# Seven products in the second layer of the fourth and fifth 512-row block of four more rounds, with the sums kept in quarters of the hidden tile

## The chip, the cores and the metric

The kernel runs on one core of a Trainium2 chip. The metric is the device time in microseconds (us) of one execution; the median of several is compared. Within the core, PE is TensorE (matrix products), DVE is VectorE, ACT is ScalarE, POOL is GpSimd and SP is SyncE, which here only issues transfers.

## What is computed

The input x has 8 batches of 2496 rows of 256 numbers. Each batch goes through a two-dimensional Fourier transform of which the real part is kept; then each of the 19968 rows is given to one of eight experts, and passes through that expert's two layers:

```python
X = np.fft.fft(x, axis=1)
X = np.fft.fft(X, axis=2)
x = X.real.reshape(B * S, D)
logits = x @ w_gate
expert_idx = np.argmax(logits, axis=1)
...
h = np.maximum(x_sorted[lo:hi] @ w1[e], 0.0)
y_sorted[lo:hi] = h @ w2[e]
...
return gate_w[:, None] * y
```

D is 256, there are 8 experts, and the hidden width F is 1024. All of it is in fp32. gate_w is the softmax probability of the chosen expert.

## The kernel before

**Stages.** Per batch, `first` folds and transforms along the sequence, `regroup` and `second` finish the transform, `route` picks the expert of each row and its place, and `send` scatters rows (with GpSimd's indirect transfers) into a buffer in HBM, `Xs`, sorted by expert. The experts work on blocks of rows of one expert. The blocks come in rounds (`rounds`, L132): round 0 has two of 256 and four of 128 rows, round 1 four of 256, round 2 three of 512, rounds 3 to 6 five of 512 each, round 7 five of 512, then seven of 256 and twenty-one of 128. While round b works, the transform of batch b+1 is woven in.

**The order of the work.** All engines run in the order in which the program issues. The main loop (L954 to 982) takes one step of `experts` at a time; each step reports a share of work, and per share some steps of the transform (`side`) and some scatters are issued. From round 3 on, transform steps are dealt only in the second layer of a block (the first reports `full`), and so fast that they are used up about three fifths through the round; the fourth and fifth block have PE to themselves. Scatters of `send` are still issued in the fourth block. A block counts 15 units, 7 in the first and 8 in the second layer, whichever way the second is done.

**Seven products.** From round 3 on, `seven` (L610) makes the first layer of a 512-row block, and of the 256-row blocks of round 7, by seven products of quarters in place of eight (Strassen's scheme in Winograd's form). The weights' side needs four differences (`Left`, L555), the rows' side four (`right`, L571, called from `turn`, L580). Per half of the hidden quarters (g is 0 or 1; one pass for 256 rows) the products go to five banks of PSUM, a to e, in the order 0, 5, 6, 4, 1, 3, 2. ACT copies bank a into p1, DVE adds: u2 = p1 + b, u3 = u2 + d, h22 = u3 + c, h21 = u3 + e, h12 = u2 + c; h11 is bank a after product 1. ACT takes the maximum with zero of each. The hidden tile hT has one buffer. Between the evictions, `step` takes one piece of pending DVE work: first the block's `chores`, then the next block's `Left`.

**The second layer.** Plain blocks (L840 to 851) take each 128 rows in turn: eight products of 128x128 by 128x256 into bank b or d, then ACT scales by the gate (L849) and POOL scatters the rows to the output. In round 7 the 512- and 256-row blocks take `lower` (L657): again seven products, now with the hidden quarters on the left and quarters of the second weights on the right. What it needs of the hidden side (s1, s2, s4 and the difference of h22 and h21) are four `chores` per half, made after the maximum, in tiles that share buffers with the input's (tag "xq"). The differences of the second weights are made by `below` (L605) in the block before, by POOL for a 512-row block and by DVE for a 256-row one. Sums p1, u2, u3 and the output y have tiles of their own. Which blocks take it, `quartered` (L197) says: all `halved` blocks of round 7.

The expert's weights (1 MB a layer) are loaded per block by SP, up to three blocks ahead; rows are fetched for the next two. The first layer's input of the next block is turned (DVE transposes, ACT negates, DVE makes the four differences) during the second layer of the block before.

## Time and profile before

| | |
|---|---|
| median of 3 runs | 1286.0 us (1285.17 to 1287.41) |
| the profiled execution: its time | 1297.33 us |
| its span, first to last instruction | 1295.5 us |
| granted TensorE clock, mean | 0.971 |
| output tiles scaled in plain blocks (L849) | 129, 473 ns each |
| scatters to the output / into Xs | 163 / 160, about 1.0 us each on POOL |
| HBM traffic over the span | 193 GB/s |

The profile is of one execution. Its busy times say how long each engine had an instruction in work; a group of instructions is named by its line, engine and tiles, with count and mean. A matrix product appears as two records. L222 is the helper through which nearly all products are issued, so these groups are told apart by the tiles' names: a to e are the banks of the seven products, ph and py those of plain first and second layers. "The chain" is the work followed back from the last instruction, at each step to what released it. Lines quoted with a start, a length and a name are from the chain or from the instructions in order of time.

### The profile page before, as it was taken

To read this page: it belongs to the slowest core of one execution; us is meant where nothing else is said; L and a number is where in the kernel's file an instruction comes from. 1 tells how busy PE (TensorE), PEld (TensorE's weight loads), DVE (VectorE), ACT (ScalarE), POOL (GpSimd) and SP (SyncE) were. 2 spreads that over 40 slices of the span, in tenths; PEclk is the share of its full clock that TensorE was granted. 3 is DMA by queue.
4 is the path that set the end of the run, shared out by engine and by line. 5 is a ranking of instruction groups with operands and counts; after the bars stand their busy time and mean duration, and the time that the engine had idled before them with its cause. 6 is when DMAs were issued, how large, how long until landed. Compare 5 with 4: busy or idle time off the path is not lost.

```text
span 1295.5 us, 20735 instructions
## 1 busy us (share of the span) xinstructions
PE 1237.7 (96%) x7003; PEld 1090.5 (84%) x7003; DVE 700.5 (54%) x1772; ACT 423.4 (33%) x1059; POOL 360.6 (28%) x355
## 2 busy tenths in 40 slices
PE   6769899899999999999999999999999999999997
PEld 4658788687688888888888888888889999999996
DVE  4554145244256655566356655467488774444662
ACT  1423133132244333443234333343333332222222
POOL 0244304314411531135111531145364221111112
PEclk6869999999999999999999999999999999999998
DMA  8877857726636853456433744344355237777776
GB/s 240 275 237 270 310 205 254 276 84 201 201 114 176 277 152 110 141 150 242 120 102 127 241 128 149 98 135 146 107 151 164 90 113 288 276 265 273 290 294 241
DMA packets 134023, 249.75 MB, mean 193 GB/s; under 512 B 85065, under 2 KB 99891, under 8 KB 114332
## 3 DMA queue, kind: packets, MB, share of 16 engines
q1 hardware_dynamic: 117143, 203.33, 48.3%
q0 software_dynamic: 15888, 42.14, 9.0%
q10 hardware_dynamic: 885, 2.94, 0.7%
q8 instruction: 57, 0.93, 0.3%
q14 instruction: 50, 0.41, 0.1%
HBM read 194.97 MB, written 54.83 MB: 193 GB/s over the span
## 4 chain that ended last, share of the span: by engine, by line
PE 70%; issue 18%; DMA 4%; POOL 3%; DVE 2%; another core or an unknown queue 2%; ACT 1%; SPq 0%; POOLq 0%; ACTq 0%; DVEq 0%
PE py L222 28%; PE a L222 7%; PE c L222 7%; PE ph L222 6%; PE p L222 5%; PE d L222 4%; PE b L222 4%; PE s L222 3%; PE e L222 3%; POOL out_dram L237 3%; DMA xq<-in_x_dram 2%; PE pt L595 1%; DMA Xs<-rows,pi 1%; DMA xb<-Xs 0%
## 5 line engine op out<-in xcount | busy, mean ns | idle before, releaser
L222 PE MATMUL py<-w_sb,hT 128*128 128x256 f32 x2016 | 455.9, 381 | 6.5 <-DVE hT L808 3.9
L222 PEld LDWEIGHTS py<-w_sb,hT 128*128 128x128 f32 x2016 | 379.5, 191 | 57.2 <-DVE hT L808 4.3
L237 POOL DMA_INDIRECT out_dram<-y,ro x163 | 160.8, 986 | 729.2 <-ACT y L849 497.9
L237 POOL DMA_INDIRECT Xs<-rows,pi x160 | 163.3, 1020 | 198.3 <-ACT pi L469 103.6
L222 PE MATMUL ph<-xT,w_sb 128*128 128x128 f32 (+2 forms) x992 | 172.4, 329 | 8.5 <-DVE hT L808 6.7
L222 PEld LDWEIGHTS ph<-xT,w_sb 128*128 128x128 f32 x992 | 136.1, 193 | 34.1 <-issue 17.2
L849 ACT ACTIVATE y<-py,xb 128x256 f32<-128x256 f32 x129 | 61.0, 473 | 313.5 <-PE py L222 271.6
L222 PE MATMUL a<-xT,w_sb 128*128 128x256 f32 (+1 forms) x512 | 117.5, 356 | 0.0
L808 DVE TENSOR_SCALAR hT<-ph 128x512 f32<-128x512 f32 x43 | 29.7, 691 | 161.9 <-issue 79.7
L633 DVE TENSOR_TENSOR u<-p,b 128x512 f32<-128x512 f32 x57 | 39.2, 687 | 132.9 <-PE b L222 96.7
L222 PEld LDWEIGHTS a<-xT,w_sb 128*128 128x128 f32 x512 | 89.2, 190 | 10.3 <-issue 0.2
L643 ACT ACTIVATE hT<-a 128x512 f32<-128x512 f32 x57 | 34.0, 597 | 151.2 <-PE a L222 133.6
L410 DVE COPY lg<-p 128x16 f32<-128x16 f32 x80 | 13.9, 174 | 121.0 <-ACT zs L407 117.5
L222 PE MATMUL s<-xq,w 104*112 104x256 f32 (+2 forms) x208 | 62.9, 427 | 11.1 <-DVE xq L299 10.9
L810 ACT ACTIVATE hT<-ph 128x512 f32<-128x512 f32 x55 | 32.8, 597 | 98.2 <-PE ph L222 71.0
L222 PEld LDWEIGHTS p<-table,t 120*128 120x128 f32 x352 | 54.3, 204 | 12.3 <-issue 6.6
L222 PE MATMUL p<-table,t 120*128 120x120 f32 (+1 forms) x352 | 58.2, 290 | 3.8 <-issue 2.7
L222 PE MATMUL c<-xT,ws 128*128 128x256 f32 (+1 forms) x256 | 59.1, 358 | 2.3 <-issue 1.7
L222 PE MATMUL p<-table,zz 128*128 128x145 f32 (+1 forms) x320 | 56.8, 302 | 3.8 <-issue 2.0
L222 PE MATMUL d<-xT,w_sb 128*128 128x256 f32 (+1 forms) x256 | 58.8, 357 | 0.0
L222 PE MATMUL e<-xs,w_sb 128*128 128x256 f32 (+1 forms) x256 | 58.7, 356 | 0.0
L222 PE MATMUL b<-xs,ws 128*128 128x256 f32 (+1 forms) x256 | 58.7, 356 | 0.0
(148 smaller groups left out, 1739.1 us busy)
## 6 DMA issues: line engine op xcount, KB each, us to landing
w_sb<-in_moe_w_dram SPq DMA_DIRECT2D x132, 1024.0 KB
xq<-in_x_dram SPq DMA_DIRECT2D x24, 896.0 KB
xb<-Xs SPq DMA_DIRECT2D x100, 128.0 KB
Td<-t SPq DMA_DIRECT2D x18, 448.0 KB
t<-Td SPq DMA_DIRECT2D x8, 768.0 KB
t<-Td SPq DMA_DIRECT2D x8, 640.0 KB
xb<-Xs SPq DMA_DIRECT2D x25, 129.0 KB
Td<-t ACTq DMA_DIRECT2D x6, 448.0 KB
```

Source lines behind the costliest of these rows:

```text
L222: nc.tensor.matmul(o, lhsT=lhsT, rhs=rhs, start=start, stop=stop, **kw)
L237: return unordered(pool.indirect_dma_start(out=dst, out_offset=bass.IndirectOffsetOnAxis(ap=idx, axis=0), in_=rows, in_offset=None, bounds ...
L410: vec.tensor_copy(lg[:, k:k + 2], p3[:, NY:NY + 2 * E].rearrange("p (m e) -> p m e", m=2))
L595: nc.tensor.transpose(pt[:, c, t], xb[:, 2 * h + t, c:D:2], ident[:])
L633: vec.tensor_tensor(u2[:], p1[:], b[:], op=add)
L643: act.activation(h11, a[:], ACTF.Relu)
L808: vec.tensor_scalar(o, ph[:], 0.0, None, op0=ALU.max)
L810: act.activation(o, ph[:], ACTF.Relu)
L849: act.activation(y[:], py[:], ACTF.Copy, scale=meta[:, i, 1:2])
```

## The change

- `quartered` now also takes the position of a block in its round: the fourth and fifth 512-row block of rounds 3 to 6 make the second layer by seven products as well. That is eight blocks more than the twelve of round 7.
- In `seven`, for every block that uses it, p1, u2 and u3 have no tiles any more: they are put where h11, h12 and h21 come to lie later. In a quartered block h21 isn't passed through ACT's maximum; DVE takes it in a fused operation that makes s1 and the difference of h21 and h22 (whose sign is turned; the weights' difference with it). s2 is then written over h22 once product 0 of the second layer has read it, and s4 over h12 once product 1 has.
- `below` becomes the class `Below`. Its four differences are made in the block itself, one after each of the first four products of its first layer, by POOL for 512 rows and DVE for 256.
- In `lower` the sums p1, u2, u3 live in the halves of the output tiles. The next block's input is turned after s4, u2 and u3 instead of at three fixed steps, and bank b is added after product 4 instead of after product 6. A last bare yield is added.
- Output tiles y are three pairs of 128 rows in place of six single ones, for all blocks. The planner's tiles have one buffer in place of two, but for `gone`.

```diff
-def quartered(b, size):
-    return halved(b, size) and b == B - 1
+def quartered(b, size, at):
+    return halved(b, size) and (b == B - 1 or at >= 3)
...
-            return cp.tile([1, *dims], dt, tag="p_" + name, name="p_" + name, bufs=2)
+            return cp.tile([1, *dims], dt, tag="p_" + name, name="p_" + name, bufs=2 if name == "gone" else 1)
...
-    def below(w, eng):
-        ws2 = sp.tile([128, 3, FC // 2, H], F32, tag="t4", name="ws2")
-        return right(ws2, *(w[:, 4 * f:4 * f + 4, k * H:(k + 1) * H] for f in (1, 0) for k in range(2)), eng=eng)
-    def seven(size, l, r, hT, step, after):
+    class Below:
+        def __init__(self, w, eng):
+            ws2 = bp.tile([128, 3, FC // 2, H], F32, tag="ws2", name="ws2", bufs=1)
+            o = [ws2[:, k] for k in range(3)]
+            b11, b12, b21, b22 = (w[:, 4 * f:4 * f + 4, k * H:(k + 1) * H] for f in (1, 0) for k in range(2))
+            self.eng, self.all = eng, (b11, b21, b22, o[2], o[0], o[1], b12)
+            self.due = deque([(o[0], b12, b11), (o[1], b22, o[0]), (o[2], b21, o[1]), (b12, b12, b22)])
+        def step(self):
+            if self.due:
+                o, p, q = self.due.popleft()
+                self.eng.tensor_tensor(o, p, q, op=sub)
+    def quarters(hT, size):
+        th, half = size // 2, FC // 2
+        return [hT[:, k * half:(k + 1) * half, t * th:(t + 1) * th] for k in range(2) for t in range(2)]
+    def seven(size, l, r, hT, both, step, ends):
...
         for g in range(half // fp):
             a, b, c, d, e = (pse.tile([128, fp, th], F32, tag=k, name=k) for k in "abcde")
-            p1, u2, u3 = (bp.tile([128, fp, th], F32, tag=n, name=n, bufs=1) for n in ("p1", "u2", "u3"))
-            h11, h12, h21, h22 = (hT[:, k * half + g * fp:k * half + (g + 1) * fp, t * th:(t + 1) * th]
-                                  for k in range(2) for t in range(2))
+            h11, h12, h21, h22 = (q[:, g * fp:(g + 1) * fp] for q in quarters(hT, size))
             product(g, 0, a)
-            act.copy(p1[:], a[:])
+            act.copy(h11, a[:])
             yield
             product(g, 5, b)
-            vec.tensor_tensor(u2[:], p1[:], b[:], op=add)
+            vec.tensor_tensor(h12, h11, b[:], op=add)
             yield
             product(g, 6, d)
-            vec.tensor_tensor(u3[:], u2[:], d[:], op=add)
+            vec.tensor_tensor(h21, h12, d[:], op=add)
             yield
             product(g, 4, c)
-            vec.tensor_tensor(h22, u3[:], c[:], op=add)
+            vec.tensor_tensor(h22, h21, c[:], op=add)
             step()
             yield
             product(g, 1, a, False)
@@ -644,17 +657,20 @@
             act.activation(h22, h22, ACTF.Relu)
             yield
             product(g, 3, e)
-            vec.tensor_tensor(h21, u3[:], e[:], op=add)
-            act.activation(h21, h21, ACTF.Relu)
+            vec.tensor_tensor(h21, h21, e[:], op=add)
+            if not both:
+                act.activation(h21, h21, ACTF.Relu)
             yield
             product(g, 2, c, False)
-            vec.tensor_tensor(h12, u2[:], c[:], op=add)
+            vec.tensor_tensor(h12, h12, c[:], op=add)
             act.activation(h12, h12, ACTF.Relu)
-            after(h11, h12, h21, h22, slice(g * fp, (g + 1) * fp))
+            ends(g)
             step()
             yield
...
-        p1, u2, u3 = (bp.tile([128, nt, H], F32, tag=n, name=n, bufs=1) for n in ("p1", "u2", "u3"))
+            for i in range(nt):
+                act.activation(y[k][:, i, lo:hi], y[k][:, i, lo:hi] if src is None else src[:, i], ACTF.Copy,
+                               scale=gate[:, k * nt + i])
+
+        def plus(o, p):
+            vec.tensor_tensor(o, o, p[:], op=add)
         a, b, c, d = (bank(k) for k in "abcd")
-        one, two = y[:, nt:2 * nt], y[:, 0:nt]
+        p1, u2, u3, high = (y[k][:, 0:nt, h * H:(h + 1) * H] for k, h in ((1, 0), (1, 1), (0, 0), (0, 1)))
         product(0, a)
-        act.copy(p1[:], a[:])
+        act.copy(p1, a[:])
+        s2()
+        if nt == 1:
+            turn_some()
         yield
         product(3, b)
         yield
         product(1, a, False)
+        s4()
+        step()
+        turn_some()
+        yield
+        product(5, c)
+        vec.tensor_tensor(u2, p1, c[:], op=add)
         scaled(1, 0, H, a)
+        if nt == 2:
+            turn_some()
+        yield
+        product(6, d)
+        vec.tensor_tensor(u3, u2, d[:], op=add)
         step()
-        yield
-        product(5, c)
-        vec.tensor_tensor(u2[:], p1[:], c[:], op=add)
-        yield
-        product(6, d)
-        vec.tensor_tensor(u3[:], u2[:], d[:], op=add)
-        vec.tensor_tensor(two[:, :, 0:H], u3[:], b[:], op=add)
-        step()
+        turn_some()
         yield
         c = bank("c")
         product(4, c)
-        vec.tensor_tensor(two[:, :, H:], u3[:], c[:], op=add)
-        vec.tensor_tensor(u2[:], u2[:], c[:], op=add)
+        vec.tensor_tensor(high, u3, c[:], op=add)
+        plus(u3, b)
+        plus(u2, c)
         scaled(0, 0, D)
-        send_rows(0, nt)
+        send_rows(0)
         step()
         yield
         d = bank("d")
         product(2, d)
-        vec.tensor_tensor(one[:, :, H:], u2[:], d[:], op=add)
+        plus(u2, d)
         scaled(1, H, D)
-        send_rows(nt, 2 * nt)
+        send_rows(1)
         step()
         yield
+        yield
...
-            both = quartered(b, size)
+            both = quartered(b, size, at)
+            below = None
             if both:
-                th, r2 = size // 2, rest
-                s12 = xp.tile([128, 2, FC // 2, th], F32, tag="xq", name="s12", bufs=3)
-                s4 = xp.tile([128, FC // 2, th], F32, tag="xq", name="s4", bufs=3)
-                l2 = [hT[:, 4 * f:4 * f + 4, t * th:(t + 1) * th] for t, f in ((1, 1), (1, 0))]
-                l2 += [s4, hT[:, 0:4, 0:th], s12[:, 0], s12[:, 1], hT[:, 4:8, 0:th]]
-
-            def after(h11, h12, h21, h22, at):
+                s1 = bp.tile([128, FC // 2, size // 2], F32, tag="s1", name="s1", bufs=1)
+                h11, h12, h21, h22 = quarters(hT, size)
+                below = Below(w2_sb, pool if size == BIG else vec)
+                fp = 1024 // size
+                parts = [slice(lo, lo + fp) for lo in range(0, FC // 2, fp)]
+
+            def ends(g):
                 if both:
-                    for o, p, q, op in ((s12[:, 0, at], h21, h11, add), (s12[:, 1, at], s12[:, 0, at], h22, sub),
-                                        (h21, h22, h21, sub), (s4[:, at], h12, s12[:, 1, at], sub)):
-                        chores.append(lambda o=o, p=p, q=q, op=op: vec.tensor_tensor(o, p, q, op=op))
+                    part = parts[g]
+                    for o, q, op in ((s1, h11, add), (h21, h22, sub)):
+                        chores.append(lambda o=o[:, part], p=h21[:, part], q=q[:, part], op=op:
+                                      vec.scalar_tensor_tensor(o, p, 0.0, q, op0=ALU.max, op1=op))
 
             if halved(b, size):
-                for _ in seven(size, left.all, xT, hT, step, after):
+                for _ in seven(size, left.all, xT, hT, both, step, ends):
+                    if both:
+                        below.step()
                     yield 0.5, True
                 while chores:
...
-                if follow[1] == BIG and quartered(*follow[:2]):
-                    rest = below(got[0][1], pool)
             if both:
-                y = xp.tile([128, BIG // 128, D], F32, tag="t1", name="y4")
-
-                def send_rows(lo, hi):
-                    for i in range(lo, hi):
-                        put_row(out, ro[:, i:i + 1], y[:, i], NT - 1, "out")
-
-                for i, _ in enumerate(lower(size, l2, r2, y, meta[:, :, 1:2], send_rows,
-                                            left.step if follow and halved(*follow[:2]) else lambda: None)):
-                    if i in (0, 2, 4):
-                        xT = next(turned, xT)
+                y = [bp.tile([128, 2, D], F32, tag="y", name="y", bufs=3) for _ in range(2)]
+
+                def send_rows(k):
+                    for i in range(n // 2):
+                        row = k * n // 2 + i
+                        put_row(out, ro[:, row:row + 1], y[k][:, i], NT - 1, "out")
+
+                def turn_some():
+                    nonlocal xT
+                    xT = next(turned, xT)
+
+                def s2():
+                    for part in parts:
+                        vec.tensor_tensor(h22[:, part], s1[:, part], h22[:, part], op=sub)
+
+                def s4():
+                    for part in parts:
+                        vec.tensor_tensor(h12[:, part], h12[:, part], h22[:, part], op=sub)
+
+                for _ in lower(size, (h22, h12, h12, h11, s1, h22, h21), below.all, y, meta[:, :, 1:2], send_rows,
+                               turn_some, s2, s4, left.step if follow and halved(*follow[:2]) else lambda: None):
                     yield 1, False
-                n = 0
-            for i in range(n):
+            for i in range(0 if both else n):
                 xT = next(turned, xT)
                 py = pse.tile([128, D], F32, tag="bd"[i % 2], name="py")
...
-                y = bp.tile([128, D], F32, tag="y", name="y", bufs=6)
-                act.activation(y[:], py[:], ACTF.Copy, scale=meta[:, i, 1:2])
-                put_row(out, ro[:, i:i + 1], y[:], NT - 1, "out")
+                if i % 2 == 0:
+                    y = bp.tile([128, 2, D], F32, tag="y", name="y", bufs=3)
+                act.activation(y[:, i % 2], py[:], ACTF.Copy, scale=meta[:, i, 1:2])
+                put_row(out, ro[:, i:i + 1], y[:, i % 2], NT - 1, "out")
...
-            if follow and follow[1] == BLK and quartered(*follow[:2]):
-                rest = below(got[0][1], vec)
```

More of the change, by code (lines that the diff above doesn't have):

```diff
@@ L646, in seven, with lower @@
             product(g, 3, e)
-            vec.tensor_tensor(h21, u3[:], e[:], op=add)
-            act.activation(h21, h21, ACTF.Relu)
+            vec.tensor_tensor(h21, h21, e[:], op=add)
+            if not both:
+                act.activation(h21, h21, ACTF.Relu)
             yield
             product(g, 2, c, False)
-            vec.tensor_tensor(h12, u2[:], c[:], op=add)
+            vec.tensor_tensor(h12, h12, c[:], op=add)
             act.activation(h12, h12, ACTF.Relu)
-            after(h11, h12, h21, h22, slice(g * fp, (g + 1) * fp))
+            ends(g)
             step()
             yield
-    def lower(size, l, r, y, gate, send_rows, step):
+    def lower(size, l, r, y, gate, send_rows, turn_some, s2, s4, step):
         nt = size // 256
@@ L672, in scaled @@
         def scaled(k, lo, hi, src=None):
-            for i in range(k * nt, (k + 1) * nt):
-                act.activation(y[:, i, lo:hi], y[:, i, lo:hi] if src is None else src[:, i - k * nt], ACTF.Copy,
-                               scale=gate[:, i])
-        p1, u2, u3 = (bp.tile([128, nt, H], F32, tag=n, name=n, bufs=1) for n in ("p1", "u2", "u3"))
+            for i in range(nt):
[3 more added lines that the diff above has]
+            vec.tensor_tensor(o, o, p[:], op=add)
         a, b, c, d = (bank(k) for k in "abcd")
-        one, two = y[:, nt:2 * nt], y[:, 0:nt]
+        p1, u2, u3, high = (y[k][:, 0:nt, h * H:(h + 1) * H] for k, h in ((1, 0), (1, 1), (0, 0), (0, 1)))
         product(0, a)
-        act.copy(p1[:], a[:])
+        act.copy(p1, a[:])
+        s2()
+        if nt == 1:
+            turn_some()
         yield
@@ L685, in lower @@
         product(1, a, False)
-        scaled(1, 0, H, a)
+        s4()
         step()
+        turn_some()
         yield
         product(5, c)
-        vec.tensor_tensor(u2[:], p1[:], c[:], op=add)
+        vec.tensor_tensor(u2, p1, c[:], op=add)
+        scaled(1, 0, H, a)
+        if nt == 2:
+            turn_some()
         yield
         product(6, d)
-        vec.tensor_tensor(u3[:], u2[:], d[:], op=add)
-        vec.tensor_tensor(two[:, :, 0:H], u3[:], b[:], op=add)
+        vec.tensor_tensor(u3, u2, d[:], op=add)
         step()
+        turn_some()
         yield
@@ L706, in lower @@
         product(2, d)
-        vec.tensor_tensor(one[:, :, H:], u2[:], d[:], op=add)
+        plus(u2, d)
         scaled(1, H, D)
-        send_rows(nt, 2 * nt)
+        send_rows(1)
         step()
         yield
+        yield
     def experts(todo):
-        xbs, got, xT, used, left, rest = [], [], None, None, None, None
+        xbs, got, xT, used, left = [], [], None, None, None
         @contextmanager
```

## The prediction

> **What bounds the kernel now.** I read the page's busy shares first, then the busy time by stretch of the eight blocks that the change touches, then the chain of waits through one such block and through a block of the last round, which already runs the scheme that is now to be used.
>
> ```profile
> span 1295.5 us, 20735 instructions
> ## 1 busy us (share of the span) xinstructions
> PE 1237.7 (96%) x7003; PEld 1090.5 (84%) x7003; DVE 700.5 (54%) x1772; ACT 423.4 (33%) x1059; POOL 360.6 (28%) x355
> ```
>
> TensorE (PE) is busy 96% of the span and no other engine over 54%. That is an average, so the stretches: the fourth and fifth block of rounds 3 and 4.
>
> ```profile
> core 0: us, PE busy (x) PEld busy (x) DVE busy (x) ACT busy (x) POOL busy (x), PEclk, DMA share, GB/s
> 450.00:475.88 25.88, 25.88 (x121) 22.78 (x120) 12.19 (x21) 9.03 (x23) 11.05 (x11) 1.00 0.42 130
> 475.88:501.78 25.90, 25.90 (x121) 22.80 (x120) 12.19 (x21) 8.42 (x16) 3.88 (x4) 1.00 0.40 122
> ```
>
> Columns: stretch, length, then busy time of PE, weight loads, VectorE (DVE), ScalarE (ACT), GpSimd (POOL). PE is busy the whole block; DVE, ACT and POOL are under half; DMA is 40% used and the clock is full. Only PE work counts here. The same holds in rounds 5 and 6 (the eight stretches sum to 207.14 us, all PE). The chain through the fourth block:
>
> ```profile
> 460.50 0.86 PE e L222 x4
> 461.37 0.86 PE c L222 x4
> 462.23 13.81 PE py L222 x64
> 476.04 0.86 PE a L222 x4
> ```
>
> The second layer ("py") is 64 records in one piece, 13.81 us, 215.8 ns each; the first layer's seven products before it are 14 pieces of 0.86. A 512-row block of the last round, where the second layer already takes seven products:
>
> ```profile
> 976.86 1.78 PE a L222 x16
> 978.64 1.79 PE b L222 x16
> 980.43 1.79 PE a L222 x16
> 982.22 1.79 PE c L222 x16
> 984.00 1.79 PE d L222 x16
> 985.79 1.79 PE c L222 x16
> 987.58 1.79 PE d L222 x16
> ```
>
> 112 records in 12.51 us, 111.7 ns each: seven products, but of half-width records that cost more than half. So the price of the new scheme is measured, not guessed.
>
> **What the skill says.** (1) SBUF — State Buffer, "SBUF: two separate sides": VectorE with two SBUF inputs and a GpSimd operation that reads SBUF take the shared port pair as a lock, and the loser waits for the whole instruction. The trace agrees: the sums at L792 have a median of 0.69 us, but 1.76 where they overlap a GpSimd sum (953.39, 955.07). (2) GPSIMD Engine Reference, "3.1 Elementwise": a two-input sum is about twice as slow there; the trace has 1.29 to 1.62 against 0.69 for 128x512. (3) VectorE: DVE Perf Modes, the errata section: an fp32 two-input operation takes (N+151)/0.96 ns, 691 for N=512; the trace has 687.
>
> **The change, part by part.** Offsets T+ are from the start of a block's second layer.
>
> *PE.* Per changed block 64 x 215.8 ns = 13.81 us go and 7 x 1.787 = 12.51 come: -1.30. Two blocks in each of rounds 3, 4, 5, 6 make eight: **-10.4 us**, all on the chain.
>
> *New waits in the second layer.* The differences "s2" and "s4" are now written over quarters that PE has just read, so VectorE waits for product 0 and for product 1. Queued behind s2 is nothing that PE needs before s2 itself; behind s4 stand a step of the next block's first-layer sums, a transpose, and u2, which frees bank c. From the trace: block of sums ends about T+2.0 (h12 starts 0.2 after T, three starts 0.60 apart); product 0 ends T+1.9; s2 in two parts ends T+3.3, wanted at T+5.4 (product 5). Product 1 ends T+5.5; s4 to 6.8, step 7.4, transpose 8.0, u2 (0.42) 8.4, wanted at T+8.9 (product 4 reuses bank c). Slack 2.1 and 0.5: nothing on the path. If cover failed by one blocked 1.76 us instruction, the cost is about 0.6.
>
> *End of the second layer.* `right` (four sums, 1.9 us with its wait for ScalarE's negation) now stands before the read of bank b too; b is free at about T+12.9, wanted at T+13.4. Bank d is freed last, about T+14.2, wanted T+14.2. In the last round d is the one that shows: the third first-layer product took 1.01 instead of 0.86 at 991.09. The whole of such loss is in the distance between second layers of the last round: 951.64, 976.70, 1001.48, 1026.08, 1050.67 give 25.06, 24.78, 24.60, 24.59, against 12.09 + 12.51 = 24.60: mean loss 0.16, greatest 0.46. I take 0.16 x 8 = **+1.3 us**, and zero and 0.46 as ends.
>
> *Sums during the first layer.* Two fused maximum-and-add per half replace one ScalarE maximum each (2 x 0.63 us less) and, in the last round, two of four sums. The trace has no 128x512 form of this fused operation between SBUF tiles. Bounds: 0.60 (start-to-start of a plain sum; no gain is possible, since it is added work) and 1.76 (a blocked sum). Taken 0.69: the small fused form at L504 has 0.30 and the plain one of about the same size 0.31. DVE gains some 8 us per block, to 20 of 24.6; it is covered by PE, as in the last round.
>
> *Weights' differences.* Four GpSimd sums (1.29 + 1.62 + 1.27 + 1.27 = 5.45 us) now run within the block's own first layer. In the fourth block they queue behind the last output scatter (ends 451.9) and share the queue with about three row scatters of 1.27: done near 460, while product 3 needs the third of them at 462 + 1.8. In the fifth block four output scatters come first, to about T'-5.7 (T' its second layer): done near T'-0.2, product 3 at T'+1.8. Slack 2 us. They hold later row scatters up by up to 5.5 us; the fetch of the next round's first rows, on SP's queue, follows the last scatter (463.98; fetch at 466.74) and is first used some 28 us later. Weights fetched behind it on that queue have as long. Cost nothing.
>
> *256-row blocks.* Their four differences move from the block before into the first layer, between evictions. Seven products of 0.89: u2 needs b at +1.95, u3 d at 2.84, h22 c at 3.74; with starts 0.60 apart h22 ends at 5.15, and the seventh product, which adds onto c, wants it at 5.36. s2 ends about 9.1, wanted at 9.17. Just enough: 0 to 0.4 us each; I take 0.1 x 6 = **+0.6**. The first of the seven gains: in the trace its differences held u2 up (1063.71 to 1066.44) and the seventh product waited 0.69: **-0.7**.
>
> *Rest.* Output tiles in three pairs in place of six singles: each scatter starts within 2.4 us of its tile in the trace, a pair comes back after three blocks at least 20 us later in the early rounds and about 14 in the last; nothing. Planner tiles with one buffer are used by DVE alone, in order. The bare last yield keeps a block at 15 units, so the side work is dealt out as before.
>
> Sum: -10.4 + 1.3 + 0.6 - 0.7 = -9.2. The profiled execution took 1297.3 (span 1295.5): 1288.1 expected. It is 11.3 above the median of the runs, which is 1286.0; the same -9.2 gives about **1277.0**.
>
> **Rivals.** *Cover too thin* (GpSimd and DVE block each other, or evictions come late): every changed block loses 0.46 as at 951.64, and six 256-row blocks 0.4: 8 x 0.84 - 2.4 = 4.3 less, 1281.7. For it: slacks of 0.2 and 0.5. Against: three of four distances lose under 0.2.
>
> *A long wait goes too.* The last round's first block loses 2.39 in its first layer (937.16 to 951.64 is 14.48, not 12.09):
>
> ```profile
> 946.01 0.58 ACT p L630
> 946.60 4.37 another core or an unknown queue
> 950.96 0.02 issue
> ```
>
> If a new layout removes it and nothing else is lost: -10.4 - 0.7 - 2.4, 1272.5. Nothing in the profile says it would.
>
> *Slower.* The same wait is the price of the first seven-product second layer after a plain block, and now comes in each changed block's second half of the first layer: 2.39 - 1.14 = +1.25 x 8, 1296. It decides from 1.14 us per block. Only in the fourth blocks it gives +0.4: no change. Against: at that place DMA is 95% busy and scatters of padding run; in the changed blocks DMA is at 40%, and the three later blocks of the last round have none.
>
> **Chances.** Forecast 0.64, thin cover 0.21, wait gone 0.06, slower 0.05, fourth blocks only 0.04. The range 1272 to 1283 takes in the first three, with the unknown costs, and leaves 0.09 out. About 0.2%, 2.6 us, is what a measurement of this kernel tells from none: faster 0.91, same 0.04, slower 0.05.
>
> **What would show it.** Right: the plain output scalings of L849 fall from 129 to 97 (32 row tiles less); the stretches of those blocks last 24.6 to 24.9; the chain there has seven pieces of 1.79. Wrong: a gap of PE before products 5, 4 or 3, or pieces named as waits in the first layer; 256-row blocks over 12.7 us; or GpSimd's differences ending after T+1.8.

## The result, and the profile after

The changed kernel takes **1284.1 us** (median of 16 runs, 1280.4 to 1286.3) where the kernel before takes 1287.2 beside it (16 runs, 1283.2 to 1290.3): ratio 0.9973, 95% interval 0.9962 to 0.9985. It is faster by 3.1 us; 9 were forecast, in a range of 1272 to 1283. The profiled execution took 1283.3 (span 1281.5).

First the page of the changed kernel, its span and busy shares:

```profile
span 1281.5 us, 21743 instructions
## 1 busy us (share of the span) xinstructions
PE 1224.9 (96%) x7387; PEld 1092.0 (85%) x7387; DVE 768.7 (60%) x1884; ACT 408.0 (32%) x1050; POOL 403.9 (32%) x387
```

PE has 12.8 us less work and 384 records more (eight times 112 in place of 64); VectorE has 68 us more, GpSimd 43 more. None of that tells whether PE still waits. Hence the stretches of the fourth and the fifth block of round 3, with the columns of before (here and in the stretch used below, a block is counted from its second product to the second product of the next):

```profile
core 0: us, PE busy (x) PEld busy (x) DVE busy (x) ACT busy (x) POOL busy (x), PEclk, DMA share, GB/s
439.96:466.17 26.21, 24.85 (x170) 23.06 (x169) 21.68 (x33) 7.64 (x21) 13.87 (x12) 1.00 0.38 102
466.17:490.77 24.60, 24.60 (x170) 23.15 (x169) 19.90 (x36) 7.75 (x18) 9.30 (x8) 1.00 0.42 130
```

The fifth block does what was forecast: 25.90 became 24.60, PE busy throughout. The fourth became *longer*, 26.21, and for 1.36 of it PE has nothing to do. Rounds 4, 5 and 6 repeat this (fourth blocks 26.14, 26.13, 26.13; fifth 24.59 to 24.60). The chain through the fourth block of round 3 shows where, in the second half of its first layer:

```profile
444.43 0.88 PE c L222 x4
...
445.94 1.15 DVE s L821
447.08 2.44 issue
449.52 0.68 DVE hT L646
...
451.83 1.13 PE c L222 x4
452.96 1.78 PE a L222 x16
```

Before, this place was an unbroken row of pieces of 0.86. Now the chain leaves PE: it runs through L821, the new fused sum for s1, then through the evictions u2, u3 and h22 behind it (L646, L649, L652), and PE's seventh product starts at 451.83 where 450.3 was its turn. VectorE's instructions there, in order of time (start, length, engine, line, operation):

```profile
445.94 3.66 DVE L821 SCALAR_TENSOR_TENSOR s<-hT 128x512 f32<-128x512 f32 x1
449.52 0.67 DVE L646 TENSOR_TENSOR hT<-hT,b 128x512 f32<-128x512 f32 x1
```

GpSimd's, in the same stretch:

```profile
445.52 0.99 POOL L237 DMA_INDIRECT Xs<-rows,pi  x1 [0.15 <-issue]
446.54 1.27 POOL L618 TENSOR_TENSOR ws<-w_sb,ws 128x512 f32<-128x512 f32 x1
447.77 1.27 POOL L618 TENSOR_TENSOR w_sb<-w_sb 128x512 f32<-128x512 f32 x1
```

An operation of 0.69 us took 3.66. It began beside a row scatter and ended at 449.60, 0.56 after the second of two sums of weights that GpSimd had queued behind that scatter. The fourth blocks of rounds 4, 5 and 6 have the same at 592.10, 738.18 and 878.19, 3.58 each. The group of these fused sums shows it as a greatest value only; the median, 686 ns, is blameless.

**Sums by stretch.** Profiled span against profiled span is 14.0 less, but 10.9 of that lies ahead of round 3 (counted as above, it starts at 355.5 before and at 344.6 after), which the change doesn't touch; the forecast had marked that execution as 11.3 above the median. From the start of round 3 to the start of the last 256-row block it is 901.0 before and 896.0 after: **-5.0**, and this stretch is used below ("the stretch"). It repeats well: 895.97 in a second trace of the changed kernel. Its parts:

| part | forecast | measured |
|---|---|---|
| 64 records become 112, eight blocks | -10.4 | -10.4 |
| losses at the end of the second layer | +1.3 | 0.0 |
| wait in the first layer, four fourth blocks | 0 | +6.2 |
| 256-row blocks, six | +0.6 | +1.7 |
| first 256-row block's wait | -0.7 | -0.95 |
| last round's first block (27.44 to 26.05) | 0 | -1.4 |
| last round's third block (24.78 to 24.59) | 0 | -0.2 |
| sum | -9.2 | -5.0 |

The row of the last round's first block is two things in one. Where nothing waits, such a block takes 24.59. The kernel before loses 2.85 there, of which the long wait that the prediction showed is 2.39; the changed kernel loses 1.46, and its chain leaves PE as in the fourth blocks. An eviction (L652) starts 0.35 late, with no releaser named; VectorE's sum at L569 behind it, begun at 927.19 beside a scatter with a GpSimd sum behind that, then takes 2.48, and the next, at L821, 1.62. With half of the change, or without row scatters in the fourth blocks, the block takes 24.59 (both below). So the old wait is gone, which no part of the forecast had, and the same collision as in the fourth blocks stands in its place. In five blocks together the collision costs about 6.2 + 1.46 = 7.7 us.

### The profile page after: what moved, and what is told of

Read it like the earlier page. It is cut to its first block, busy times and chain, and to the rows that moved or that the text cites. A ratio compares the mean times of both kernels' runs of the same rounds, so it can differ in the third digit from the quotient of the medians.

```text
span 1281.5 us, 21743 instructions
## 1 busy us (share of the span) xinstructions
PE 1224.9 (96%) x7387; PEld 1092.0 (85%) x7387; DVE 768.7 (60%) x1884; ACT 408.0 (32%) x1050; POOL 403.9 (32%) x387
## 4 chain that ended last, share of the span: by engine, by line
PE 70%; issue 17%; DMA 4%; DVE 4%; POOL 3%; ACT 1%; POOLq 0%; SPq 0%; DVEq 0%; ACTq 0%
PE py L222 20%; PE c L222 10%; PE a L222 10%; PE d L222 7%; PE ph L222 6%; PE p L222 6%; PE b L222 5%; PE e L222 3%; PE s L222 3%; POOL out_dram L237 2%; DMA xq<-in_x_dram 1%; DMA xb<-Xs 1%; DMA Td<-t 1%; PE pt L595 1%; POOL Xs L237 1%
## 5 line engine op out<-in xcount | busy, mean ns | idle before, releaser
L222 PE MATMUL py<-w_sb,hT 128*128 128x256 f32 x1504 | 342.7, 380 | 0.0
L222 PEld LDWEIGHTS py<-w_sb,hT 128*128 128x128 f32 x1504 | 281.8, 191 | 36.4 <-issue 0.5
L889 ACT ACTIVATE y<-py,xb 128x256 f32<-128x256 f32 x97 | 45.9, 473 | 243.1 <-PE py L222 242.7
L646 DVE TENSOR_TENSOR hT<-hT,b 128x512 f32<-128x512 f32 x57 | 39.1, 686 | 72.0 <-PE b L222 46.7
L222 PE MATMUL d<-w_sb,hT 128*128 128x128 f32 x528 | 65.5, 275 | 0.0
L222 PE MATMUL a<-w_sb,hT 128*128 128x128 f32 x528 | 65.5, 275 | 0.0
L222 PEld LDWEIGHTS a<-w_sb,hT 128*128 128x128 f32 x528 | 63.2, 192 | 0.7
L222 PEld LDWEIGHTS p<-table,t 120*128 120x128 f32 x352 | 54.4, 204 | 10.4 <-issue 2.6
L222 PEld LDWEIGHTS d<-w_sb,hT 128*128 128x128 f32 x528 | 62.2, 192 | 0.0
## 6 DMA issues: line engine op xcount, KB each, us to landing
xq<-in_x_dram SPq DMA_DIRECT2D x24, 896.0 KB, 8.6
```

The source lines that it names most:

```text
L222: nc.tensor.matmul(o, lhsT=lhsT, rhs=rhs, start=start, stop=stop, **kw)
L646: vec.tensor_tensor(h12, h11, b[:], op=add)
L889: act.activation(y[:, i % 2], py[:], ACTF.Copy, scale=meta[:, i, 1:2])
```

## The experiments

Theory A: **the port pair.** VectorE's new sums with two SBUF inputs meet GpSimd's new sums of weights in the fourth blocks, behind row scatters; PE waits some 1.55 us in each. Rivals: VectorE simply has too much to do there (B), or the seven products in the second layer themselves are at fault (C). Each run's times are compared with the kernel before on the same chip, whose median was 1286 to 1308 us on the chips used; the length of the fourth blocks hardly depends on the chip, so it carries the reading, with the stretch beside it.

**The changed kernel again.** No edit.

> The changed kernel once more, on the chip of the next three, as their reference. Both theories: about 3 us under the kernel before (ratio 0.9965 to 0.9985), with the first fused sum in each of the four fourth blocks lasting about 3.6 us and TensorE waiting 1.4 to 1.6 us at the last product of that block's first layer. If the long sums are an accident of one execution, they are elsewhere or gone here.

Ratio 0.999 (0.9976 to 1.0003), stretch 895.97. The blocks repeat within 0.02 us, and the long sums stand where they stood. The time does not repeat so well (1284.0 beside 1286.5): the interval includes 1, so that on this chip the gain isn't told from none.

**Fifth blocks only.**

```
-        return ... (b == B - 1 or at >= 3)
+        return ... (b == B - 1 or at >= 4)
```

> Only the fifth blocks (four) make the second layer by seven products; the fourth blocks go back to plain. Lock theory (in the fourth blocks VectorE's fused sum waits behind GpSimd's queue, and eats the gain): each fourth block now costs 0.3 us more than a plain one, so this is 1.2 us faster than the changed kernel, ratio to before 0.995 to 0.997. Rival (the fourth blocks do gain their 1.3 us and the loss lies in the 256-row blocks and the tail): 4 x 1.3 = 5 us slower than the changed kernel, ratio 1.000 to 1.002.

Ratio 0.9955 (0.9941 to 0.9968), stretch 893.5: with half of the change undone the kernel gains more than with all of it. The four fourth blocks are a net loss of 0.23 to 0.32 each as changed (25.90 here), 1.0 together. The other 1.46 us of the difference lie in the last round's first block, 24.59 here for 26.05: here its sum at L569 starts 0.34 earlier in the block, ends before the scatter beside it does, and isn't held (0.71).

**The weights' differences on VectorE** for 512 rows too, so that GpSimd makes no such sums.

```
-                below = Below(w2_sb, pool if size == BIG else vec)
+                below = Below(w2_sb, vec)
```

> The four differences of the second weights are made by VectorE in the 512-row blocks too, so GpSimd has no sums left anywhere. Lock theory: no fused sum over 0.75 us, fourth blocks at 24.6 to 24.8 us, 5 to 6 us faster than the changed kernel (ratio to before 0.992 to 0.994), if the 2.8 us more on VectorE per block stay covered. Rival, chain too long (the fused sums in VectorE's order between the evictions are what is late, whoever makes the differences): VectorE has more to do in the same place, so the wait at the last product of the first layer stays or grows, 1 us or more in each of 13 blocks: 5 us or more slower than the changed kernel (ratio over 1.001).

Ratio 0.9976 (0.9966 to 0.9985), stretch 895.0. Fourth blocks: 24.65 three times, 25.22 in round 6. No fused sum is long any more, although the scatters are there and VectorE has four sums more: that speaks against B and C in the fourth blocks. But the blocks that follow a quartered one become 25.25, because there VectorE has the last sums of the block before, the four new ones and the evictions in one row, and the seventh product waits 0.39. So VectorE has no room for the sums in general, and the gain is lost again.

**No fused sums in the first layer**: VectorE makes no two-input SBUF sum until the first layer is done.

```
             def step():
+                if both and size == BIG and early:
+                    return
                 if chores:
...
                     yield 0.5, True
+                early = False
                 while chores:
```

> In quartered 512-row blocks VectorE makes no sum with two inputs from SBUF during the first layer: the four fused sums wait until its end, and the next block's weight sums are made in the second layer. GpSimd's queue is unchanged. Lock theory: nothing left for GpSimd to hold up but what comes after its sums; fourth blocks at 24.6, 5.5 to 6.5 us faster than the changed kernel (ratio to before 0.9915 to 0.9935). Rival (GpSimd's sums hold up evictions too, or the sums put off are late for product 5): no gain, the wait moves to product 5 of the second layer, ratio 0.996 to 0.999.

Ratio 0.9945 (0.9932 to 0.9959), stretch 891.0. Fourth blocks of rounds 3 to 5: 24.59, with scatters and GpSimd's sums in place. The fourth of round 6 is 25.75: the sums now come late, pieces of the planner get in between s2 and s4, and u2 (L712) waits behind them, 0.89 for PE.

**No row scatters in the fourth blocks' first layer**; they are issued later.

```
-                    yield 0.5, True
+                    yield 0.5, 2 if both and b < B - 1 and at == 3 else True
...
-            if b >= LATE and room >= ROOM:
+            if b >= LATE and room >= ROOM and full != 2:
```

> No row scatter is issued while a fourth block of rounds 3 to 6 is in its first layer; the seven come in its second layer. GpSimd's four sums stay there. If what holds VectorE is a scatter with sums right behind it, the first fused sum now meets one GpSimd sum at most (1.9 us or less instead of 3.6), TensorE's wait at the last product of that layer falls from 1.4 us to 0.3 or less, and the kernel is 4 to 6 us faster than the changed one (ratio to before 0.9925 to 0.995). If GpSimd's sums alone hold it that long, with or without scatters between, the fused sum stays over 2.5 us and the gain is under 2 us.

Ratio **0.9927** (0.9903 to 0.995), stretch 889.8. All four fourth blocks 24.59, and the last round's first block too; the fifth block of round 5 became longer, 26.00. The same fused sum, in VectorE's order:

```profile
445.23 1.33 DVE L821 SCALAR_TENSOR_TENSOR s<-hT 128x512 f32<-128x512 f32 x1
446.48 0.69 DVE L646 TENSOR_TENSOR hT<-hT,b 128x512 f32<-128x512 f32 x1
```

and GpSimd's sums around it:

```profile
443.05 2.96 POOL L618 TENSOR_TENSOR ws<-w_sb,ws 128x512 f32<-128x512 f32 x2
445.97 1.72 POOL L618 TENSOR_TENSOR w_sb<-w_sb 128x512 f32<-128x512 f32 x1
```

The collision is still there, but here VectorE gets its turn between two sums: it waits for the one in work (till 446.0), and then the next is the one that stretches, 1.72 for 1.27. This is the 1.33 that the schedule can hide; 3.6 it can't. A repeat on another chip:

> The changed kernel without row scatters in the first layer of the fourth blocks, again: stretch 889.8 us as on the other chip, 0.9927 of the kernel before in time within 0.002.

Ratio 0.9904 (0.9879 to 0.9928), fourth blocks 24.59 and 24.60, stretch 893.1, where 889.8 was expected; the 3.3 us above the other chip's lie in the first 256-row block (1.45), the fifth of round 6 (0.8) and the first two of round 7. So the fourth blocks repeat from chip to chip, and the stretch as a whole doesn't within 3 us.

So three ingredients are needed: the scatter, GpSimd's sum behind it, and VectorE's two-input sum. Take any of them away and the fourth block of rounds 3 to 5 is 24.59 to 24.65. B and C fall for these blocks, and **A holds in its three ingredients**; that the port pair is the means is inferred from the page that the prediction cites, and no run isolates it.

How sharp the condition is can be read off all eighteen traces. VectorE's 128x512 sums of two SBUF tiles that began beside a scatter: with no GpSimd sum within 0.06 us behind the scatter, 807 of them, at most 0.72 us, 540 of these reaching past the scatter's end; with one behind it, but due to end at least 0.2 us before the scatter's end, 84, again at most 0.72; due to end after the scatter, with one behind it, **32, of which each waited**, and ended 0.56 after the last sum of the row: 1.86 to 2.52 with one sum, 3.56 to 3.68 with two. Evictions, which read one of their inputs from PSUM, are spared: 184 of them (128x512 too) were due to end after a scatter with a GpSimd sum behind it, and none took more than 0.69. Of each kind of sum one: beside a scatter alone (459.94 to 460.91, kernel before)

```profile
460.29 0.69 DVE L569 TENSOR_TENSOR w_sb<-w_sb 128x512 f32<-128x512 f32 x1
```

and beside a scatter with a sum behind it (changed kernel, first block of round 7; here it is a plain sum, so the fused operation isn't what matters)

```profile
926.84 0.97 POOL L237 DMA_INDIRECT out_dram<-y,ro  x1 [0.31 <-issue]
927.83 1.28 POOL L618 TENSOR_TENSOR ws<-w_sb 128x512 f32<-128x512 f32 x1
927.19 2.48 DVE L569 TENSOR_TENSOR ws<-w_sb 128x512 f32<-128x512 f32 x1
```

**The fourth blocks' differences made by GpSimd in the block before.**

```
-                below = Below(w2_sb, pool if size == BIG else vec)
+                below = rest or Below(w2_sb, pool if size == BIG else vec)
...
+                if follow[1] == BIG and not both and quartered(*follow[:2], follow[3]):
+                    rest = Below(got[0][1], pool)
+                    for _ in range(4):
+                        rest.step()
```

> One part of the change undone, for the four fourth blocks alone: the differences of their second weights are made by GpSimd in the second layer of the block before, as the last round's were before. Lock theory: nothing is left of GpSimd's sums in the fourth block's first layer, fused sums at 0.7 us, fourth blocks at 24.6 us, and the third blocks (plain, 26.3) as they were if VectorE's small routing operations there stay covered: 5 to 6.3 us faster than the changed kernel, ratio to before 0.9915 to 0.994. Rival (the same lock then holds up the transposes and routing of the third block): the 1.5 us reappear there, no gain.

Ratio 0.9964 (0.9951 to 0.9977), stretch 893.0. Fourth blocks 24.60 in rounds 3 to 5, as A has it; 27.84 in round 6, a miss, and a hit for the rival in that one block. VectorE has planner steps ahead of that block's evictions in the changed kernel as well, in the same order. But its small operations of routing and planning in the third block now meet GpSimd's four sums (853.75 to 858.96), and four of them take 4.5 us together in place of 0.7. One of them, in the changed kernel and here:

```profile
859.39 0.17 DVE L447 TENSOR_SCALAR su<-su 128x10 f32<-128x10 f32 x1
853.66 1.42 DVE L447 TENSOR_SCALAR su<-su 128x10 f32<-128x10 f32 x1
```

So the planner steps end late, the first eviction starts 6.0 us after the block's first product in place of 2.0, and the seventh product waits 2.98. In rounds 3 to 5 the small operations are held up as much, but no planner steps follow them into the fourth block.

**256-row blocks.** They were 0.33 late in all six (34.62 and 27.35, where 34.29 and 27.03 is the pace without a wait). The obvious suspects were the weights' differences, which now lie between the evictions. So: the same, made at the end of the block before.

```
-                below = Below(w2_sb, pool if size == BIG else vec)
+                below = rest or Below(w2_sb, pool if size == BIG else vec)
...
+            if follow and follow[1] == BLK and size == REST and quartered(*follow[:2], follow[3]):
+                rest = Below(got[0][1], vec)
+                for _ in range(4):
+                    rest.step()
```

> One part of the change undone, for six of the seven 256-row blocks: VectorE makes the differences of their second weights at the end of the 128-row block before. If it is these sums between the evictions that make s2 late for product 5, the distances between first layers of 256-row blocks return from 34.62 to 34.29 and from 27.36 to 27.05, 1.9 us in all (ratio to before about 0.996). If the fused sums or the output pairs are the cause, they stay.

Ratio 0.9981 (0.9967 to 0.9994), stretch 896.0: **nothing moved**, 34.62 and 27.35 again. The four sums did move (1081.34 to 1084.07 ahead of the block's first eviction at 1084.36), so this suspicion is wrong. Together with the absent fused sums:

> Two remedies together: no VectorE sum with two SBUF inputs during the first layer of a quartered 512-row block, and the differences for 256-row blocks after a 128-row block made before it. If the two costs are independent, 4.9 us (as the first alone gained in the trace) and 1.9 us add: 6.5 to 7 us faster than the changed kernel, ratio to before 0.991 to 0.993.

Ratio 0.9941 (0.9921 to 0.9961), stretch 891.2: what the fused sums alone give. In the changed kernel's trace the last eviction h12 (L665) is on time; what follows it, in VectorE's order:

```profile
1087.56 0.69 DVE L665 TENSOR_TENSOR hT<-hT,c 128x512 f32<-128x512 f32 x1
1088.16 0.69 DVE L821 SCALAR_TENSOR_TENSOR s<-hT 128x512 f32<-128x512 f32 x1
1088.95 0.69 DVE L821 SCALAR_TENSOR_TENSOR hT<-hT 128x512 f32<-128x512 f32 x1
1089.75 0.69 DVE L870 TENSOR_TENSOR hT<-s,hT 128x512 f32<-128x512 f32 x1
```

s2 (L870) is the third in the row, as it is written over h22, which the one ahead of it still reads; it ends at 1090.44, and product 5 starts at 1090.50, where 1090.28 was its turn. The new place of s2 sets the order. So s2 gets a place of its own, in the half of the tile that 256 rows leave unused, and is made second:

```
+            if both and size == BLK:
+                s2t = hT[:, 0:FC // 2, BLK:BLK + size // 2]
...
+                        if o is h21 and size == BLK:
+                            chores.append(lambda: vec.tensor_tensor(s2t, s1, h22, op=sub))
...
```

> The changed kernel, but in the 256-row blocks the difference s2 goes to a place of its own (an unused part of the activations' tile) and is made as the second of the three sums that follow the last eviction, not as the third, which had to wait until h22 was no longer read. Theory: in those blocks the product that uses s2 started 0.2 to 0.3 late because of this order; the cycles of 34.62 and 27.35 us go back to 34.29 and 27.05 to 27.1, which over six of them is 1.9 us: 0.9985 of the changed kernel, 0.996 of the kernel before. Rival, that the weights' differences between the evictions make them late: nothing moves.

Ratio 0.993 (0.9904 to 0.9956), stretch 895.4. The second to sixth cycle: 34.29, 34.30, 34.28, 27.03, 27.03, as the theory has it, 1.6 us together. VectorE's order in one of these blocks:

```profile
1137.06 0.69 DVE L665 TENSOR_TENSOR hT<-hT,c 128x512 f32<-128x512 f32 x1
1137.67 0.68 DVE L826 SCALAR_TENSOR_TENSOR s<-hT 128x512 f32<-128x512 f32 x1
1138.46 0.69 DVE L824 TENSOR_TENSOR hT<-s,hT 128x512 f32<-128x512 f32 x1
1139.07 0.69 DVE L826 SCALAR_TENSOR_TENSOR hT<-hT 128x512 f32<-128x512 f32 x1
```

s2 now starts 1.40 after h12, not 2.19. The first cycle is 35.65 here: on this chip and on one more the first 256-row block waited 0.9 to 1.5 us in its first layer in every kernel, the kernel before too (35.16, 35.32, 35.30). This is left out of the comparison; what holds it is not settled.

**Both cures together**, without scatters in the fourth blocks, and then in the fifth as well.

> Two cures together: no row scatters are issued in the first layer of the fourth blocks (worth 6.2 us in the traced stretch when alone), and s2 in a place of its own in the 256-row blocks (1.9 us by the theory). Expected: fourth blocks 24.6 us, cycles 34.3 and 27.1, the stretch from the start of round 3 to the last 256-row block 888, time 0.991 of the kernel before, near 1275 us.

Ratio 0.991 (0.9877 to 0.9942), stretch 890.1, of which 1.3 are that chip's first 256-row block and 0.8 the last round's second block (25.37); fourth blocks 24.59 to 24.60.

> As the run before it, but no row scatters are issued in the first layer of the fifth blocks either. With the scatters held back from the fourth blocks alone, one fifth block (round 5) had become 26.0 us. Theory: the held-back scatters met its GpSimd sums; without them there it is 24.6 us, the stretch 886.5 and the time 0.990 of the kernel before. Rival: the scatters pile up and meet the first block of the next round, which then lasts longer by as much or more; the time is 0.991 to 0.994.

Ratio 0.991 (0.9881 to 0.9938), stretch 889.3. The fifth block of round 5 stays at 26.06, a miss for both sides: the pile-up that the rival expected did not come, and the cure did not reach that block. Its differences start only behind four output and two row scatters (782.52 in the last trace), and VectorE and GpSimd sums then lengthen each other to 1.6 to 1.9. The same version beside the simpler one on a third chip:

> The best version again on this chip: no row scatters in the first layers of the fourth and fifth blocks and s2 in a place of its own. Stretch 888 us if the first 256-row block does not wait as it did on the chip of the run before (1.3 us), time 0.990 of the kernel before, about 2 us below the version beside it.

Ratio **0.9883** (0.9865 to 0.9901), 1293.3 beside 1296.2 of the version without the new place of s2 and with the fifth blocks' scatters, and 1308.1 of the kernel before; stretch 889.3. This version beats the kernel before, and its ratio lies below that of the changed kernel, which was not run on this chip. Not all of the 14.8 us are the cures': 2.9 to 5.8 are the last round's first block, 24.59 here and 27.50 and 30.41 in the kernel before (next).

**The kernel before, three times more**, for the 2.39 us wait in the last round's first block (27.44 before, 26.05 after).

> The kernel before, once more, for what its one profile showed: 2.39 us of waiting in the first layer of the last round's first block (that block lasted 27.44 us) and a start of round 3 some 10 us later than in every other profile. Theory: both belonged to that one execution. Then the block lasts 25 to 26.1 us here, round 3 starts near 346, the stretch from the start of round 3 to the start of the last 256-row block is 898.5 to 900 instead of 901.0, and the change is worth 2.5 to 4 us in the traces as in the medians. Rival: the wait is a part of the kernel before; then it is here again at 2.4 us, the stretch is 901.0, and 2 us of the change's gain in the trace are lost somewhere in the head or the tail. Time: 1.000 of the kernel before.

Ratio 1.0 (0.9983 to 1.0017), stretch 903.2, that block 29.67.

> The kernel before, one more trace. If the wait in the last round's first block varies from execution to execution, the block is here between 25.1 and 27.4 us, the stretch from the start of round 3 to the last 256-row block 898 to 901 us. If it belongs to the kernel, 27.4 us again and 901.0.

> The kernel before, a trace more on the same chip: the same two cases as for the run before it; together with it this gives the spread of that block from one execution to the next.

27.50 and 30.41; stretches 901.2 and 903.8. The block never is below 27.44, so my theory that the wait was an accident of one execution falls: it belongs to the kernel before, and on these chips it can be longer still. In the longest, PE's seventh product in the second half:

```profile
954.21 1.13 PE L222 MATMUL a<-xT,w_sb 128*128 128x256 f32 x4 [0.71 <-ACT p L630]
959.36 2.08 PE L222 MATMUL c<-xT,ws 128*128 128x256 f32 x4 [3.15 <-DVE hT L639]
```

It waits for evictions, which VectorE and ScalarE both start late, with nothing in the trace that names a releaser, while scatters of padding run and DMA is up to 99% busy (950 to 956). With the weights' differences on VectorE eight such scatters follow each other in that block as well, but from 6.3 us into it in place of 2.2, and it takes 25.25, like its neighbours; whether their time decides is not shown.

## Why the prediction was wrong

**PE, -1.30 per block: right to the digit.** Fifth blocks went from 25.90 to 24.60, in seven pieces of 1.79. Plain output scalings (L849 before, L889 after) fell from 129 to 97.

**New waits in the second layer, none: right.** s2 and s4 over quarters just read, and `right` ahead of bank b, cost PE nothing in 512-row blocks.

**End of the second layer, +1.3: too dear, it is 0.** I took the last round's mean loss of 0.16. Part of it was a loss of the old order: the last round's third block lost 0.2 less with the new.

**Weights' differences, "Cost nothing": this step failed.** Their place was right, done 10 us into the fourth block (449.04; its first product starts at 439.09), as forecast. What I checked was when the *result* was needed, slack 2 us, and that was right as well: no product waited for it. What I did not check was who is held up *while they run*. I had the collision on the page, under another heading, "one blocked 1.76 us instruction" and 0.6, and in the bound of the fused sum, 0.60 to 1.76. The trace of before had shown only sums that meet one sum. In the fourth block the queue holds scatter, sum, sum without a gap; 3.6 us, with three evictions behind it. 1.62 + 1.54 + 1.53 + 1.53 = 6.2 us, two thirds of the forecast gain. The last round's first block, whose differences moved into it too, adds 1.46. With this step falls "it is covered by PE", which the prediction said of VectorE's new sums. The sum at L821 of round 3 ended 2.97 late (449.60 for 446.63), of which PE's work hid 1.4.

The Trainium skill's SBUF — State Buffer, "SBUF: two separate sides", from which I argued, has the pair go to whichever starts first, for a whole instruction. That a whole instruction is waited for, the runs confirm (1.33 till the sum in work ends). But VectorE's sum at 445.94 began 0.60 before the GpSimd sum of 446.54 and still came after it and the next: behind a scatter the measurement decides against "first", as far as the profile's start times on GpSimd can be trusted. Without a scatter the page is right: in the trace of before a VectorE sum that began 0.10 ahead of GpSimd's took no longer than usual, and GpSimd's did.

```profile
952.78 0.68 DVE L792 TENSOR_TENSOR hT<-hT 128x512 f32<-128x512 f32 x1
952.88 1.72 POOL L576 TENSOR_TENSOR ws<-w_sb,ws 128x512 f32<-128x512 f32 x1
```

**256-row blocks, +0.1 each: it is 0.33, for another reason.** "s2 ends about 9.1, wanted at 9.17" counted starts 0.60 apart. Where a sum writes over what the one ahead of it reads, or reads its result, they start 0.79 apart (1088.16, 1088.95, 1089.75), and s2 had been put third. The weights' differences, for which I had priced up to 0.4, cost nothing: no change without them, and with them in place, but s2 in a place of its own, the pace without a wait is reached.

**First 256-row block, -0.7: -0.95.** Right in these two traces: the seventh product no longer waits. On the two slower chips, though, it waits 1.2 to 1.3 in the kernels with the change and 0.8 to 0.9 in the kernel before, so this gain isn't one that every chip has.

**The rivals.** *Thin cover* is nearest in the gain (4.3, measured 3.1) and half right in the mechanism: GpSimd and VectorE do block each other, but in the first layer, in four of the eight blocks and in one of the last round. *Slower* named the right place, the second half of the first layer, and the right sign: 1.55 is more than the 1.14 from which it decides, so the fourth blocks did become slower; it had the wrong cause, and by the luck of where the scatters stand only half of its blocks. Its version "only in the fourth blocks", given 0.04, named the blocks that slowed. *Long wait goes too* came true, and by luck, as no step of the prediction led to it: the block lost 2.85, and the collision put 1.46 back. Without this 2.85 the stretch would have fallen by 2.2, not by 5.0.

**What stays open.** Why the change ends the long wait in the last round's first block was not settled: no trace with the change, in whole or in part, has a wait over 1.5 there, and no run isolates what removes it. Why a scatter ahead of GpSimd's sums takes VectorE's turn away isn't shown either. And the stretch fell by 5.0 where the times fell by 3.1 (1.9 to 4.9 by the interval). In the profiled pair the end after the stretch is 1.9 longer (39.0 to 40.95), which would close the sum, but over all traces this end varies from 38.7 to 41.0 without order, and on one chip the times fell by more than the stretch (11.9 beside 9.4), not by less. I take it for the spread of start and end, which is not shown.

## What to carry to other kernels

When work is moved onto a second engine, ask not only when its result is due but whom it holds up while it runs, and look at what stands directly ahead of and behind it in its queue: here the same sums were free in the fifth block and cost 1.55 us in the fourth, because of the scatters ahead of them in the queue. A change applied in two places can gain in one and lose in the other; look at each stretch alone, and try each alone, before believing the total. And a value that is written in place inherits the order of the old one's readers: count the start-to-start distance of sums that depend on each other, not that of free ones.

## What the runs showed of the hardware

- A 128x512 VectorE sum of two SBUF tiles that would reach past the end of a scatter with GpSimd sums directly behind it ends 0.56 us after the last of these: 1.9 to 2.5 us with one, 3.6 to 3.7 with two (32 of 32). A scatter without such a sum behind it doesn't delay it (807, at most 0.72), and an eviction with one input in PSUM isn't delayed in the same place (184, at most 0.69). Why is not shown.
- The fused maximum-and-add, 128x512 between SBUF tiles, takes 0.69 us, as long as the plain sum: at this size the second operation is free.
- Of two VectorE sums of 128x512 in a row, one that reads the other's result, or writes over what it reads, starts 0.79 us after it, an independent one 0.60.
